# One core, attention at two scales and two feed-forward layers: v's tiles loaded per quarter of the partitions, block tails kept in SBUF, two weight tiles queued early, some decode and split work moved off VectorE

## The chip, the core and the metric

The kernel runs on one core of a Trainium2 chip. The metric is the device time of one execution in microseconds (us); of several executions the median is given. About 0.2% is what a measurement of this kernel can tell from no change.

## What is computed

The inputs q, k and v have 4 batches, 8 heads, 576 positions and 64 values a head. The attention is the sum of two: one over positions that are means of four neighbours (144 of them, full softmax, its output repeated four times), and one over a band of the seven nearest positions. Its output, 2304 tokens of 512 values, goes through two gated feed-forward layers.

```python
q_d, k_d, v_d = (t.reshape(B, H, S // 4, 4, D).mean(axis=3) for t in (q, k, v))
out_up = np.repeat(sm_attn(q_d, k_d, v_d), 4, axis=2)
mask = np.abs(pos[:, None] - pos[None, :]) < 4
out_local = softmax(where(mask, scale * q @ k.T, -1e9)) @ v
x = (out_up + out_local) as (B * S, H * D)
x = (sigmoid(x @ w_gate) * (x @ w_val)) @ w_out          # 512 -> 1536 -> 512
h = x @ w_in; x = (h * sigmoid(1.702 * h)) @ w_out2      # 512 -> 2048 -> 512
```

The weights arrive as 64-bit numbers (float64 bits) and are decoded on the chip.

## The kernel before, in words

**Units of work.** The tokens are cut into five blocks: block 0 to 3 are the first 512 tokens of each batch, block E gathers the last 64 tokens of each batch (its *tail*), 256 in all. The attention is cut into 16 *jobs*, one per batch and pair of heads (hp 0 to 3); jobs 0 to 3 make the input of block 0, jobs 4 to 7 that of block 1, and so on. A `Values` object holds v for two jobs (half of a batch's columns).

**A job** (`Job`). It loads qt and kt (288 KB each). `pools` makes the means of four on GpSimd (L462, L464) and of v on VectorE (L431, L433, from vg). `scores` multiplies in bands (TensorE L494), adds the mask (VectorE L501 into sc), takes the maximum, the exponential (ScalarE L512), normalizes and transposes (L521 into tt). `down` does the coarse attention (L534, L541, L549, L563), `down_t` transposes it (L578, L583 into pdt). `values` multiplies by v (L606 with vt, L614 with vd) and `combine` adds both parts into xf (L633), splits xf into a rounded high part xhi (ScalarE L638) and a rest xlo (VectorE L640), and, for the second half of the columns, writes the tail of 64 columns from xf to the DRAM buffer x1d.

**v's tiles** (`Values.load`). vt holds v in overlapping windows: 24 tiles of 32 rows, four of them on the four quarters of the partitions (32 partitions each) and six (g) behind each other. Before, one transfer brings one g for all quarters: eight transfers a half, of 96 to 128 partitions, and two small ones of 27.

**A feed-forward block** (`visit`). For each f (12 in layer 1, 16 in layer 2) `hidden` and `result` multiply: a group is three matmuls (L713, L714, L715: high by high, low by high, high by low), four groups for each of three weight tiles, 144 groups a block in layer 1. For block 0 each of the 36 weight tiles is loaded (512 KB), decoded (`bits`: scale, shift, or; `signed`: sign, into w32) and split into whi (ScalarE L677) and wlo (L679, VectorE for block 0, L679 on VectorE or GpSimd later). Blocks 1 to 3 use the decoded tiles again. Layer 2's tiles are decoded during block 3 and block E.

**What sets the order.** Every instruction is entered into a plan with its engine, an assumed duration, a due time and what it reads and writes. `Plan.order` then sets each engine's order by a simulation with these numbers; the engines run that order as it stands, each waiting at its own head. All loads and stores go through SP's queue in that order; a transfer waits for the one eight places before it. TensorE's gaps that the plan foresees are filled with matmuls on zeros (L885, `warm`).

Of the kernel before, what the change touches and what calls it, by code (L numbers as in the profile page):

```python
# [10 lines left out]
F32 = mybir.dt.float32  # L11
# [5 lines left out]
ALU = mybir.AluOpType  # L17
# [200 lines left out]
def tile_multiscale_attention_gated_ffn(  # L218
# [69 lines left out]
    ring("th", 2, [P, T])  # L288
    ring("ev", 2, [P, 512])
    ring("st", 2, [P, 512])  # L290
    ring("xf", 2, [P, HALF])


    wslots = ring("w", 3 * NF1, [P, 512], I32, wpool)
    aslots = []
    for nm, n, shape in (("qt", 2, [P, S + 12]), ("kt", 2, [P, KPAD + S + 5]), ("vt", 2, [P, NG, VC]),
                         ("sc", 2, [P, 2, NG, NU]), ("pt", 2, [P, 2, NG, 32]), ("tt", 2, [P, 2, NG, 32]),
                         ("vg", 1, [GH, 2, 4, VC]), ("half", 1, [P, G, 2]),
                         ("qd", 2, [P, G]), ("kd", 2, [P, G]), ("vd", 2, [GH, 2, VC]),
                         ("nm", 2, [P, 2, NG]), ("sm", 2, [P, 2, NG]), ("pd", 2, [GH, 2, 2, G]),  # L300
                         ("nmd", 2, [GH, 4]), ("smd", 2, [GH, 4]), ("pdt", 2, [GH, 2, 2, G]), ("up", 2, [P, G])):
# [19 lines left out]
        return [Buf(Slot(dram.tile([P, NK, T], F32, name=f"{name}_{j}", tag=f"{name}_{j}")))  # L321
                for j in range(len(blocks))]

    x1d, x2d = (dram_blocks(n) for n in ("x1d", "x2d"))


    warm = sb.tile([P, P], BF16, name="warm", tag="warm")
# [72 lines left out]
    class Values:  # L400
# [6 lines left out]
        def load(self):  # L407
            b, c = self.b, slice(self.c0, self.c0 + VC)
            self.vg, self.vt, self.vd = buf("vg"), buf("vt"), buf("vd")

            hp = self.job.hp
            d, after = (self.job.t0 - 3000.0, self.job.t0 - 12000.0) if b else (4500.0 * hp, 4500.0 * hp)
            for kh in range(2):
                dma(self.vg.t[:, kh], v[b, kh * 4 * GH:(kh + 1) * 4 * GH, c].rearrange("(g r) d -> g r d", r=4),
                    GH * 4 * VC * 4, [], [(self.vg, kh)], d, after)
            d, after = (self.job.due(0.2), self.job.t0 - 9000.0) if b else (4500.0 * hp + 3000.0, 6000.0 * hp)
            for g in range(NG):
                i0, i1 = g == 0, 4 - (g == NG - 1)
# [17 lines left out]
    class Job:  # L436
# [189 lines left out]

        def combine(self, a, z, s, xf, first, xh, xl):
            b, hp, up = self.b, self.hp, self.up
            m = z - a
            hi = min(z, T)  # L630
            at = self.due(0.9 if first else 1.0)
            part = (hp, first)
            op("dve", dve_ns(m), lambda: nc.vector.tensor_tensor(  # L633
                out=xf.t[:, :m].rearrange("p (g r) -> p g r", r=4),
                in0=s.t[:, :m].rearrange("p (g r) -> p g r", r=4),
                in1=up.t[:, a // 4:z // 4, None].to_broadcast([P, m // 4, 4]), op=ALU.add),
               [s, up], [xf], at)
            op("act", act_ns(hi - a), lambda: nc.scalar.copy(xh.t[:, hp, a:hi], xf.t[:, :hi - a]),  # L638
               [xf], [(xh, part)], at)
# [169 lines left out]

    def load_x(layer, j, t):  # L810
        n = width(j)
        src = (x1d if layer == 1 else x2d)[j]
        new_x((layer, j))
        direct.discard((layer, j))
        hi, lo = xs[layer, j]
        for k in range(NK):
            st = buf("st")
            reads = [(src, k)]
            if layer == 1:
                reads = [(src, (k, y)) for y in (range(B) if j == E else (True, False))]  # L820
            dma(st.t[:, :n], src.t[:, k, :n], P * 4 * n, reads, [st], t - 8000.0 + 500 * k)
            op("act", act_ns(n), lambda k=k, st=st: nc.scalar.copy(hi.t[:, k, :n], st.t[:, :n]),
               [st], [(hi, k)], t - 3000.0 + 500 * k)
            op("pool", pool_ns(n), lambda k=k, st=st: nc.gpsimd.tensor_sub(
                lo.t[:, k, :n], st.t[:, :n], hi.t[:, k, :n].bitcast(F32)),
               [st, (hi, k)], [(lo, k)], t - 3000.0 + 500 * k)
# [98 lines left out]
```

## Time and profile before

| | |
|---|---|
| median of 3 runs | 1001.41 us (1000.36 to 1001.48) |
| the profiled execution | 1000.16 us |
| its span, first to last instruction | 998.1 us |
| mean granted TensorE clock | 0.983 |
| TensorE busy | 961.1 us (96%) |
| VectorE busy | 526.0 us (53%) |
| ScalarE busy | 414.1 us (41%) |
| GpSimd busy | 219.1 us (22%) |

Busy times of TensorE count a matmul to its modelled end, and so hide short waits. Times inside the profile are counted from the start of the span.

### The profile page before, as it was taken

The numbers are of one execution on the slowest core, as the hardware profiler recorded it, in microseconds if no ns is written. First come the engines' busy times: TensorE is split into PE (matmuls) and PEld (weight loads), VectorE is DVE, ScalarE is ACT, GpSimd is POOL, SyncE is SP. The second block draws the span as 40 slices with busy tenths as digits, with TensorE's granted clock in tenths as the row PEclk, the third lists the DMA queues.
The fourth block names the chain that finished last, engine by engine and source line by source line (L and its number), as shares of the span: only waits on it lengthen the run. The fifth ranks groups of instructions, "written<-read, shape, count | busy, mean of one in ns | idle before, by whom it ended". The sixth has DMA issues, their size and how long they took to land.

```text
span 998.1 us, 18490 instructions
## 1 busy us (share of the span) xinstructions
PE 961.1 (96%) x7611; PEld 782.6 (78%) x7611; DVE 526.0 (53%) x932; ACT 414.1 (41%) x886; POOL 219.1 (22%) x212
## 2 busy tenths in 40 slices
PE   5799999899999999999999989999999999999997
PEld 5677677778778777888889967788888888888896
DVE  4899899554344544578655689523222222322232
ACT  2546565444444444555546555323223212322222
POOL 4111201333233332255435442102002000100000
PEclk8899999799999999999999999999999999999999
DMA  6656656130112110153105145002001000100010
GB/s 178 185 186 190 195 167 172 40 101 27 51 57 69 57 32 8 66 163 103 43 1 169 44 127 177 14 1 85 1 1 50 25 1 1 53 1 1 3 40 21
DMA packets 36931, 72.40 MB, mean 73 GB/s; under 512 B 5440, under 2 KB 17648, under 8 KB 36848
## 3 DMA queue, kind: packets, MB, share of 16 engines
q1 hardware_dynamic: 36848, 71.23, 22.9%
q8 instruction: 59, 0.97, 0.4%
q14 instruction: 24, 0.20, 0.1%
HBM read 61.26 MB, written 9.96 MB: 71 GB/s over the span
## 4 chain that ended last, share of the span: by engine, by line
PE 78%; DVE 13%; DMA 5%; issue 2%; ACT 1%; SPq 0%; DVEq 0%; ACTq 0%
PE ph L713 15%; PE ph L714 14%; PE ph L715 14%; PE acc L713 10%; PE acc L714 10%; PE acc L715 10%; DMA w<-w 3%; DVE we L666 3%; PE pa L606 2%; DVE we L671 2%; DVE w L671 1%; DVE we L664 1%; DVE wlo L679 1%; PE pa L494 1%; DMA x1d<-xf 1%
## 5 line engine op out<-in xcount | busy, mean ns | idle before, releaser
L749 DVE SCALAR_TENSOR_TENSOR th<-th,ph 128x512 f32<-128x512 f32 (+1 forms) x140 | 88.5, 632 | 282.2 <-ACT th L744 205.8
L744 ACT ACTIVATE th<-ph 128x512 f32<-128x512 f32 (+1 forms) x140 | 77.5, 554 | 259.7 <-PE ph L715 259.5
L713 PE MATMUL ph<-xhi,whi 128*128 128x512 f32 (+1 forms) x480 | 183.0, 381 | 0.4 <-ACT th L744 0.4
L714 PE MATMUL ph<-xhi,wlo 128*128 128x512 f32 (+1 forms) x480 | 178.9, 373 | 2.0 <-DVE wlo L679 2.0
L715 PE MATMUL ph<-xlo,whi 128*128 128x512 f32 (+1 forms) x480 | 177.9, 371 | 0.0
L679 POOL TENSOR_TENSOR wlo<-w,whi 128x512 fp32r<-128x512 f32 x90 | 121.1, 1345 | 239.2 <-ACT whi L677 234.7
L677 ACT CAST whi<-w 128x512 fp32r<-128x512 f32 x180 | 110.8, 617 | 106.9 <-PE acc L715 41.3
L713 PE MATMUL ph<-xhi,w 128*128 128x512 f32 (+1 forms) x320 | 120.0, 375 | 1.1 <-DVE th L749 0.9
L753 DVE TENSOR_TENSOR glo<-th,ghi 128x512 fp32r<-128x512 f32 (+1 forms) x140 | 95.6, 683 | 48.1 <-ACT ghi L752 47.6
L715 PE MATMUL ph<-xlo,w 128*128 128x512 f32 (+1 forms) x320 | 119.2, 372 | 0.0
L714 PE MATMUL ph<-xhi,w 128*128 128x512 f32 (+1 forms) x320 | 119.1, 372 | 0.0
L714 PE MATMUL acc<-w,glo 128*128 128x512 f32 x288 | 114.2, 397 | 2.5 <-DVE glo L753 2.5
L713 PE MATMUL acc<-w,ghi 128*128 128x512 f32 x288 | 113.9, 396 | 1.5 <-ACT ghi L752 1.5
L715 PE MATMUL acc<-w,ghi 128*128 128x512 f32 x288 | 114.0, 396 | 0.0
L752 ACT CAST ghi<-th 128x512 fp32r<-128x512 f32 (+1 forms) x140 | 80.8, 577 | 65.7 <-DVE th L749 63.1
L713 PEld LDWEIGHTS ph<-xhi,whi 128*128 128x128 f32 x480 | 91.1, 190 | 19.0 <-issue 3.9
L714 PEld LDWEIGHTS ph<-xhi,wlo 128*128 128x128 f32 x480 | 91.3, 190 | 17.7 <-DVE wlo L679 4.3
L715 PEld LDWEIGHTS ph<-xlo,whi 128*128 128x128 f32 x480 | 91.2, 190 | 15.5
L713 PE MATMUL acc<-ghi,whi 128*128 128x512 f32 (+1 forms) x240 | 91.0, 379 | 1.0 <-DVE ev L789 0.6
L714 PE MATMUL acc<-ghi,wlo 128*128 128x512 f32 (+1 forms) x240 | 89.2, 371 | 1.5 <-DVE wlo L679 1.5
L715 PE MATMUL acc<-glo,whi 128*128 128x512 f32 (+1 forms) x240 | 88.5, 369 | 0.5 <-DVE glo L753 0.5
L679 DVE TENSOR_TENSOR wlo<-w,whi 128x512 fp32r<-128x512 f32 x90 | 69.4, 772 | 19.2 <-ACT whi L677 19.1
(99 smaller groups left out, 1264.2 us busy)
## 6 DMA issues: line engine op xcount, KB each, us to landing
w<-w SPq DMA_DIRECT2D x68, 512.0 KB
qt<-qT SPq DMA_DIRECT2D x16, 288.0 KB
kt<-kT SPq DMA_DIRECT2D x16, 288.0 KB
vg<-v SPq DMA_DIRECT2D x16, 288.0 KB
vt<-v SPq DMA_DIRECT2D x32, 128.0 KB
x2d<-ev SPq DMA_DIRECT2D x16, 256.0 KB
st<-x2d SPq DMA_DIRECT2D x16, 256.0 KB
out<-ev SPq DMA_DIRECT2D x16, 256.0 KB
```

The costliest lines, as they stand in the source:

```text
L606: nc.tensor.matmul(s.t[h * D:(h + 1) * D, q:q + NQ], vt.t[ks, g, v0 + h * D:v0 + (h + 1) * D], tt.t[ks, h, g, :NQ], start=True, stop=True, ...
L666: op("dve", 602.0, lambda: nc.vector.scalar_tensor_tensor(e.t, wv[:, :, 0], 29, e.t, op0=ALU.logical_shift_right, op1=ALU.bitwise_or), [w] ...
L671: op("dve", 602.0, lambda: nc.vector.scalar_tensor_tensor(m.t, top, -2 ** 31, e.t, op0=ALU.bitwise_and, op1=ALU.bitwise_or), [w] if m is e ...
L677: op("act", 520.0, lambda: nc.scalar.copy(hi.t, m.t.bitcast(F32)), [m], [hi], due)
L679: op(eng, ns, lambda: on.tensor_sub(lo.t, m.t.bitcast(F32), hi.t.bitcast(F32)), [m, hi], [lo], due)
L713: nc.tensor.matmul(o, lhi, rhi, start=first, stop=False)
L714: nc.tensor.matmul(o, llo, rhi, start=False, stop=False)
L715: nc.tensor.matmul(o, lhi, rlo, start=False, stop=last)
L744: op("act", act_ns(n, True), lambda h=h: nc.scalar.activation(th.t[:, :n], h.t[:, :n], AF.Tanh, scale=0.5 if layer == 1 else 1.702 / 4.0), ...
L749: op("dve", dve_ns(n), lambda: nc.vector.scalar_tensor_tensor(th.t[:, :n], th.t[:, :n], 1.0, hb[-1].t[:, :n], op0=ALU.add, op1=ALU.mult), ...
L752: op("act", act_ns(n), lambda: nc.scalar.copy(gh.t[:, :n], th.t[:, :n]), [th], [gh], t)
L753: op("dve", dve_ns(n), lambda: nc.vector.tensor_sub(gl.t[:, :n], th.t[:, :n], gh.t[:, :n].bitcast(F32)), [th, gh], [gl], t)
```

## The change

1. vt is loaded by quarter of the partitions: four transfers of 32 partitions with five or six windows each, and two small ones of 28 and 27 partitions.
2. xf goes into the pool of the attention's buffers and no longer holds the tail; the tail's 64 columns are added by an instruction of their own into an SBUF buffer `tails` for all four batches. x1d is gone: block E's input is split straight from `tails`, without loads. sc has one buffer instead of two, which makes the room.
3. The first f's three weight tiles get due times of their own (`FIRST`), and the plan puts them among the first jobs' loads.
4. The first decode step (the scaling by 2 ** -112) is always on ScalarE; before, six tiles had it on VectorE (L660). For batch 0 the subtraction that makes xlo is on GpSimd.
5. The plan assumes 617 ns instead of 520 for ScalarE's operations of 512 columns.

```diff
-    ring("xf", 2, [P, HALF])
-                         ("sc", 2, [P, 2, NG, NU]), ("pt", 2, [P, 2, NG, 32]), ("tt", 2, [P, 2, NG, 32]),
+                         ("sc", 1, [P, 2, NG, NU]), ("pt", 2, [P, 2, NG, 32]), ("tt", 2, [P, 2, NG, 32]),
...
+                         ("xf", 2, [P, HALF])):
-    x1d, x2d = (dram_blocks(n) for n in ("x1d", "x2d"))
+    x2d = dram_blocks("x2d")
+    tails = Buf(Slot(sb.tile([P, NK, B * TAIL], F32, name="tails", tag="tails")))
...
-    E_DVE = 8.0e3
+    FIRST = ((-15.0e3, 0.0), (3.5e3, 0.0), (10.0e3, 8.0e3))
...
-            for g in range(NG):
-                i0, i1 = g == 0, 4 - (g == NG - 1)
-                src = v[b, NQ * (NG * i0 + g) - 3:NQ * (NG * i0 + g) + 29, c]
+            for i in (0, 2, 1, 3):
+                g0, g1 = i == 0, NG - (i == 3)
+                row = NQ * (NG * i + g0) - 3
+                src = v[b, row:row + 32, c]
                 src = bass.AP(tensor=src.tensor, offset=src.offset,
-                              ap=[[NG * NQ * DM, i1 - i0], [DM, 32], [1, VC]])
-                dma(self.vt.t[32 * i0:32 * i1, g], src, 32 * (i1 - i0) * VC * 4, [], [(self.vt, g)], d, after)
-            dma(self.vt.t[3:NU, 0], v[b, :NU - 3, c], (NU - 3) * VC * 4, [], [(self.vt, NG)], d, after)
+                              ap=[[DM, 32], [NQ * DM, g1 - g0], [1, VC]])
+                dma(self.vt.t[32 * i:32 * i + 32, g0:g1], src, 32 * (g1 - g0) * VC * 4, [], [(self.vt, i)],
+                    d, after)
+            dma(self.vt.t[3:NU + 1, 0], v[b, :NU - 2, c], (NU - 2) * VC * 4, [], [(self.vt, 4)], d, after)
...
-            op("dve", dve_ns(hi - a), lambda: nc.vector.tensor_sub(
-                xl.t[:, hp, a:hi], xf.t[:, :hi - a], xh.t[:, hp, a:hi].bitcast(F32)),
+            eng, ns, on = ("pool", pool_ns(m), nc.gpsimd) if b == 0 else ("dve", dve_ns(m), nc.vector)
+            op(eng, ns, lambda: on.tensor_sub(
+                xl.t[:, hp, a:hi], xf.t[:, :m], xh.t[:, hp, a:hi].bitcast(F32)),
                [xf, (xh, part)], [(xl, part)], at)
             if z > T:
-                dma(x1d[E].t[:, hp, b * TAIL:(b + 1) * TAIL], xf.t[:, T - a:m], P * 4 * (z - T),
-                    [xf], [(x1d[E], (hp, b))], at)
+                op("dve", dve_ns(z - T), lambda: add(tails.t[:, hp, b * TAIL:(b + 1) * TAIL], T, z),
+                   [s, up], [(tails, (hp, b))], at)
...
-        dma(w.t, (w1 if layer == 1 else w2)[f, part], P * 4096, [], [w], due - 5000.0, due - AHEAD)
+        at, after = due - 5000.0, due - AHEAD
+        if (layer, f) == (1, 0):
+            at, after = FIRST[part]
+        dma(w.t, (w1 if layer == 1 else w2)[f, part], P * 4096, [], [w], at, after)
...
-        if due < T0 + E_DVE:
-            op("dve", 335.0, lambda: nc.vector.tensor_scalar_mul(ef, wf[:, :, 1], 2.0 ** -112), [w], [e], due)
-        else:
-            op("act", 520.0, lambda: nc.scalar.activation(ef, wf[:, :, 1], AF.Copy, scale=2.0 ** -112),
-               [w], [e], due)
+        op("act", 617.0, lambda: nc.scalar.activation(ef, wf[:, :, 1], AF.Copy, scale=2.0 ** -112),
+           [w], [e], due)
```

The order of the instructions moves on every engine. Three places matter here.

SP's queue at the start of the kernel; qt and kt are a job's q and k, vg and vt are v, w a weight tile. Before:

```order
L367 DMA qt_137<-qT 128x576
L367 DMA kt_139<-kT 128x576
L367 DMA qt_138<-qT 128x576
L367 DMA kt_140<-kT 128x576
L367 DMA vg_149<-v 72x4x256 x2
L367 DMA vt_141<-v 96x1x256
L367 DMA vt_141<-v 128x1x256 x4
L367 DMA vt_141<-v 96x1x256
L367 DMA vt_141<-v 27x256 x2
L367 DMA qt_137<-qT 128x576
L367 DMA kt_139<-kT 128x576
```

and with the change:

```order
L368 DMA qt_135<-qT 128x576
L368 DMA kt_137<-kT 128x576
L368 DMA w_79<-w 128x512
L368 DMA qt_136<-qT 128x576
L368 DMA kt_138<-kT 128x576
L368 DMA vg_146<-v 72x4x256 x2
L368 DMA vt_139<-v 32x5x256
L368 DMA vt_139<-v 32x6x256 x2
L368 DMA vt_139<-v 32x5x256
L368 DMA vt_139<-v 28x256
L368 DMA vt_139<-v 27x256
L368 DMA w_80<-w 128x512
```

The first weight tile is now the third transfer and the second one stands ahead of the second pair's qt and kt, which follow it; v's half takes six transfers instead of eight.

VectorE after the scores of the first two jobs (sc scores, sm and pt softmax, we and w the decoding of weights). Before:

```order
L510 TENSOR_TENSOR sc_144<-sc_144,nm_158 128x360
L541 TENSOR_REDUCE nmd_164<-pa_177 72x2
L541 TENSOR_REDUCE nmd_164<-pa_178 72x2
L501 TENSOR_TENSOR sc_143<-acc_171,mask 128x180
L544 TENSOR_SCALAR nmd_164<-nmd_164 72x4
L501 TENSOR_TENSOR sc_143<-acc_173,mask 128x180
L513 TENSOR_REDUCE sm_160<-pt_146 128x12
```

and with the change:

```order
L513 TENSOR_TENSOR sc_141<-sc_141,nm_155 128x360
L547 TENSOR_SCALAR nmd_161<-nmd_161 72x4
L673 SCALAR_TENSOR_TENSOR we_83<-w_79,we_83 128x512
L671 TENSOR_SCALAR we_84<-we_84 128x512
L516 TENSOR_REDUCE sm_157<-pt_143 128x12
L519 TENSOR_SCALAR sm_157<-sm_157 128x12
L520 RECIPROCAL sm_157<-sm_157 128x12
```

Where VectorE had to wait for the scores of the third job (acc_171) before it could go on with job 1's softmax, steps of the first two tiles' decoding stand now, and that softmax comes ahead of the third job's scores.

VectorE at the end of job 1's values (xf the sum, xlo its rest). Before:

```order
L633 TENSOR_TENSOR xf_99<-pa_178,up_170 128x288
L633 TENSOR_TENSOR xf_100<-acc_172,up_170 128x288
L520 TENSOR_TENSOR pt_146<-pt_146,sm_160 128x12x30
L640 TENSOR_TENSOR xlo_87<-xf_99,xhi_85 128x288
L640 TENSOR_TENSOR xlo_87<-xf_100,xhi_85 128x224
L521 STREAM_TRANSPOSE tt_148<-pt_146 128x384
```

and with the change:

```order
L638 TENSOR_TENSOR xf_168<-acc_172,up_167 128x288
L638 TENSOR_TENSOR xf_169<-acc_173,up_167 128x224
L638 TENSOR_TENSOR tails<-acc_173,up_167 128x64
L544 TENSOR_REDUCE nmd_161<-acc_170 72x2
L544 TENSOR_REDUCE nmd_161<-acc_171 72x2
L547 TENSOR_SCALAR nmd_161<-nmd_161 72x4
```

The second addition stops at column 224 and the tail has its own; the two subtractions are no longer in VectorE's list.

## Rows read from the trace of the kernel before

**Rows 1.** The page's 40 slices of the span: granted TensorE clock in tenths.

```profile
PEclk8899999799999999999999999999999999999999
```

**Rows 2.** Stretches, only the matmuls of L713: us, PE busy (count), PEld busy (count), clock, DMA share, GB/s.

```profile
48.90:191.70 142.80, 60.69 (x144) 27.98 (x145) 0.95 0.53 163
191.70:309.90 118.20, 58.13 (x144) 26.98 (x144) 1.00 0.18 55
...
429.30:526.20 96.90, 55.71 (x144) 26.96 (x145) 1.00 0.23 77
```

**Rows 3.** Stretches: us; PE, PEld, DVE, ACT, POOL busy (count); clock, DMA share, GB/s.

```profile
0.00:10.00 10.00, 6.78 (x222) 6.29 (x223) 3.77 (x18) 1.28 (x1) 7.47 (x26) 1.00 0.65 191
...
0.00:60.00 60.00, 43.76 (x1149) 37.39 (x1151) 40.91 (x113) 23.49 (x77) 14.66 (x38) 0.83 0.63 192
60.00:175.00 115.00, 108.24 (x1141) 82.97 (x1137) 109.14 (x218) 65.17 (x149) 16.83 (x17) 1.00 0.57 176
176.00:186.00 10.00, 8.51 (x75) 6.23 (x76) 7.03 (x13) 4.41 (x10) 1.46 (x1) 0.52 0.01 2
191.70:310.00 118.30, 118.30 (x1202) 94.49 (x1201) 54.03 (x105) 55.25 (x133) 42.74 (x43) 1.00 0.18 55
...
30.00:33.50 3.50, 3.33 (x51) 2.83 (x49) 3.28 (x11) 1.98 (x7) 0.00 (x0) 1.00 0.96 296
45.50:48.50 3.00, 0.96 (x36) 0.96 (x40) 2.96 (x8) 1.82 (x6) 0.27 (x1) 0.53 0.26 84
```

**Rows 4.** The chain of work that ended last: start us, us, what.

```profile
3.68 6.01 DMA vg<-v
...
14.59 6.92 DMA kt<-kT
...
33.90 7.87 DMA x1d<-xf
...
59.40 0.67 DVE xlo L640 x2
...
166.53 9.52 DMA w<-w
```

**Rows 5.** Waits of VectorE, 0 to 60 us (three rows) and 60 to 192 us: total, times, longest.

```profile
DVE sc L501 <- PE acc L494: 6.5, 1, 6.5
DVE sc L501 <- PE pa L494: 3.4, 1, 3.4
DVE xf L633 <- DMA x1d<-xf: 2.3, 1, 2.3
...
DVE we L664 <- ACT we L662: 6.8, 3, 3.9
```

**Rows 6.** SP in order of time, 159 to 168 us: start us, us, issue.

```profile
159.52 6.91 SPq L367 DMA_DIRECT2D vt<-v  x5
166.53 1.30 SPq L367 DMA_DIRECT2D w<-w  x1
```

**Rows 7.** VectorE and GpSimd in order of time, 169.5 to 180 us.

```profile
170.36 1.35 POOL L679 TENSOR_TENSOR wlo<-w,whi 128x512 fp32r<-128x512 f32 x1 [7.63 <-ACT whi L677]
170.48 1.78 DVE L679 TENSOR_TENSOR wlo<-w,whi 128x512 fp32r<-128x512 f32 x1
...
177.96 0.69 DVE L679 TENSOR_TENSOR wlo<-w,whi 128x512 fp32r<-128x512 f32 x1
```

**Rows 8.** VectorE's groups by shape, 0 to 192 us: busy us, mean ns | idle before.

```profile
L501 DVE TENSOR_TENSOR sc<-pa,mask 128x180 f32<-128x180 f32 x13 | 4.1, 336 | 3.7 <-PE pa L494 3.4 <-ACT whi L677 0.4
L640 DVE TENSOR_TENSOR xlo<-xf,xhi 128x288 fp32r<-128x288 f32 x8 | 3.6, 450 | 0.0
...
L660 DVE TENSOR_SCALAR we<-w 128x512 f32<-128x512 f32 x6 | 3.2, 538 | 1.4 <-DMA w<-w 1.3
```

**Rows 9.** GpSimd in order of time, 22 to 25 us.

```profile
22.89 0.66 POOL L462 TENSOR_TENSOR half<-qt 128x288 f32<-128x288 f32 x1
```

**Rows 10.** TensorE in order of time, 165 to 195 us; in brackets its idle time before.

```profile
177.50 0.69 PE L578 MATMUL pa<-ident,pd 72*72 72x72 f32 x4 [4.19 <-DVE sc L501]
```

More of the change, by code (lines that the diff above doesn't have):

```diff
@@ L300, in tile_multiscale_attention_gated_ffn @@
                          ("nm", 2, [P, 2, NG]), ("sm", 2, [P, 2, NG]), ("pd", 2, [GH, 2, 2, G]),
-                         ("nmd", 2, [GH, 4]), ("smd", 2, [GH, 4]), ("pdt", 2, [GH, 2, 2, G]), ("up", 2, [P, G])):
+                         ("nmd", 2, [GH, 4]), ("smd", 2, [GH, 4]), ("pdt", 2, [GH, 2, 2, G]), ("up", 2, [P, G]),
+                         ("xf", 2, [P, HALF])):
         aslots += ring(nm, n, shape, F32, apool)
@@ L416, in load @@
             d, after = (self.job.due(0.2), self.job.t0 - 9000.0) if b else (4500.0 * hp + 3000.0, 6000.0 * hp)
-            for g in range(NG):
-                i0, i1 = g == 0, 4 - (g == NG - 1)
-                src = v[b, NQ * (NG * i0 + g) - 3:NQ * (NG * i0 + g) + 29, c]
+            for i in (0, 2, 1, 3):
+                g0, g1 = i == 0, NG - (i == 3)
+                row = NQ * (NG * i + g0) - 3
+                src = v[b, row:row + 32, c]
                 src = bass.AP(tensor=src.tensor, offset=src.offset,
-                              ap=[[NG * NQ * DM, i1 - i0], [DM, 32], [1, VC]])
-                dma(self.vt.t[32 * i0:32 * i1, g], src, 32 * (i1 - i0) * VC * 4, [], [(self.vt, g)], d, after)
-            dma(self.vt.t[3:NU, 0], v[b, :NU - 3, c], (NU - 3) * VC * 4, [], [(self.vt, NG)], d, after)
+                              ap=[[DM, 32], [NQ * DM, g1 - g0], [1, VC]])
+                dma(self.vt.t[32 * i:32 * i + 32, g0:g1], src, 32 * (g1 - g0) * VC * 4, [], [(self.vt, i)],
+                    d, after)
+            dma(self.vt.t[3:NU + 1, 0], v[b, :NU - 2, c], (NU - 2) * VC * 4, [], [(self.vt, 4)], d, after)
             row = NQ * (NT - 1) - 3
-            dma(self.vt.t[96:96 + S - row, NG - 1], v[b, row:S, c], (S - row) * VC * 4, [], [(self.vt, NG + 1)],
+            dma(self.vt.t[96:96 + S - row, NG - 1], v[b, row:S, c], (S - row) * VC * 4, [], [(self.vt, 5)],
                 d, after)
@@ L628, in combine, with add @@
             b, hp, up = self.b, self.hp, self.up
-            m = z - a
             hi = min(z, T)
+            m = hi - a
             at = self.due(0.9 if first else 1.0)
             part = (hp, first)
[L633 to L638, printed above, removed]
+            def add(out, o0, o1):
+                nc.vector.tensor_tensor(
+                    out=out.rearrange("p (g r) -> p g r", r=4),
+                    in0=s.t[:, o0 - a:o1 - a].rearrange("p (g r) -> p g r", r=4),
+                    in1=up.t[:, o0 // 4:o1 // 4, None].to_broadcast([P, (o1 - o0) // 4, 4]), op=ALU.add)
+            op("dve", dve_ns(m), lambda: add(xf.t[:, :m], a, hi), [s, up], [xf], at)
+            op("act", act_ns(m), lambda: nc.scalar.copy(xh.t[:, hp, a:hi], xf.t[:, :m]),
                [xf], [(xh, part)], at)
-            op("dve", dve_ns(hi - a), lambda: nc.vector.tensor_sub(
-                xl.t[:, hp, a:hi], xf.t[:, :hi - a], xh.t[:, hp, a:hi].bitcast(F32)),
+            eng, ns, on = ("pool", pool_ns(m), nc.gpsimd) if b == 0 else ("dve", dve_ns(m), nc.vector)
+            op(eng, ns, lambda: on.tensor_sub(
+                xl.t[:, hp, a:hi], xf.t[:, :m], xh.t[:, hp, a:hi].bitcast(F32)),
                [xf, (xh, part)], [(xl, part)], at)
             if z > T:
-                dma(x1d[E].t[:, hp, b * TAIL:(b + 1) * TAIL], xf.t[:, T - a:m], P * 4 * (z - T),
-                    [xf], [(x1d[E], (hp, b))], at)
+                op("dve", dve_ns(z - T), lambda: add(tails.t[:, hp, b * TAIL:(b + 1) * TAIL], T, z),
+                   [s, up], [(tails, (hp, b))], at)
     wt = {}
@@ L675, in parts_of @@
     def parts_of(m, hi, lo, due, eng):
-        op("act", 520.0, lambda: nc.scalar.copy(hi.t, m.t.bitcast(F32)), [m], [hi], due)
+        op("act", 617.0, lambda: nc.scalar.copy(hi.t, m.t.bitcast(F32)), [m], [hi], due)
         ns, on = (602.0, nc.vector) if eng == "dve" else (1230.0, nc.gpsimd)
@@ L811, in load_x @@
         n = width(j)
-        src = (x1d if layer == 1 else x2d)[j]
         new_x((layer, j))
@@ L816, in load_x @@
         for k in range(NK):
-            st = buf("st")
-            reads = [(src, k)]
             if layer == 1:
[L820 to L826, printed above, removed]
+                st, x, reads = tails, tails.t[:, k], [(tails, (k, b)) for b in range(B)]
+            else:
+                st, reads = buf("st"), None
+                x = st.t[:, :n]
+                dma(x, x2d[j].t[:, k, :n], P * 4 * n, [(x2d[j], k)], [st], t - 8000.0 + 500 * k)
+                reads = [st]
+            op("act", act_ns(n), lambda k=k, x=x: nc.scalar.copy(hi.t[:, k, :n], x),
+               reads, [(hi, k)], t - 3000.0 + 500 * k)
+            op("pool", pool_ns(n), lambda k=k, x=x: nc.gpsimd.tensor_sub(
+                lo.t[:, k, :n], x, hi.t[:, k, :n].bitcast(F32)),
+               [*reads, (hi, k)], [(lo, k)], t - 3000.0 + 500 * k)
     def visit(v_):
```

## The prediction

> **What bounds the kernel now.** Start with the granted clock in the 40-slice view [rows 1]. It reads 8 in the first two slices (0 to 50 us), 7 in the eighth (175 to 200 us) and 9, which stands for full, everywhere else. The clock falls where TensorE stands still, so these are the places to look at.
>
> Next, how long each block of 512 tokens takes in the first layer [rows 2]. Every block is the same 144 groups of three matmuls. Block 3 has no attention beside it and takes 96.9 us, 0.67 us a group. Block 1 shares TensorE with the attention of block 2 and takes 118.2 us. Block 0 shares it with the attention of block 1, the same work, and takes 142.8 us, and it only begins at 48.9 us. So what can be saved lies before 191.7 us: 24.6 us inside block 0, and part of the 48.9 us ahead of it.
>
> Third, the engines in stretches [rows 3]. From 60 to 175 us VectorE is busy 109.14 of 115 us: it decodes the 36 weight tiles of layer 1 there, and it sets the pace. From 0 to 60 us it works only 40.91 us, so 19.1 us are idle. In block 1 TensorE is busy 118.30 of 118.30 us: from there on a microsecond won earlier is kept, and one spent on another engine costs nothing.
>
> Fourth, what VectorE waited for [rows 5] and the chain of work that ended last [rows 4]. Before 60 us: 6.5 and 3.4 us for score matmuls, 2.3 us for the write of a block tail, 1.3 us for the first weights [rows 8]. On the chain stand three transfers: kt issued at 14.59 us takes 6.92 us, the tail's write of 32 KB takes 7.87 us, a weight tile of 512 KB issued at 166.53 us takes 9.52 us.
>
> Fifth, why transfers are slow. While weights are loaded the DMA engines are 0.96 busy at 296 GB/s; while SP issues v's tiles (45.5 to 48.5 us) the DMA engines are 0.26 busy at 84 GB/s [rows 3]. A quarter of the engines carries v's tiles, and what is queued on that quarter behind them waits. The last weight tile of block 0 is issued right behind five v tiles whose issue alone took 6.91 us [rows 6].
>
> **The change, part by part.**
>
> v's tiles. Per half of v 759 KB (0.78 MB) move, 9.3 us at 84 GB/s. The new shape is in no row; its bounds are 84 and 296 GB/s, 9.3 and 2.6 us. I take the 191 GB/s of the first 10 us, in which all kinds of loads are mixed [rows 3]: 4.1 us. Ahead of kt of the second pair of jobs stand then 3.41 MB of q, k, v's groups and two weight tiles (11.5 us at 296 GB/s) and 4.1 us of v; six loads before the first v tiles (1.77 MB, 6.0 us) landed at 9.7 us (3.68 + 6.01) [rows 4], so I count from 3.7 us: 19.3 us, against 21.5 (14.59 + 6.92). VectorE's 6.5 us wait [rows 5] shrinks to some 3, since weight decode now stands in it: **-3.5 us**.
> A rule speaks against this part. The Trainium skill, page "SBUF — State Buffer", section "Door 1: The DMA port swizzle", says that a transfer to 32 partitions reaches 8 of 16 ports and measures 189 GB/s where 128 partitions measure 328. No row here shows such a transfer of v. Scaled to this case's 296 GB/s it would be 171 GB/s and 4.6 us a half, and the sum would be 0.5 us smaller.
>
> Tails on the chip. 16 writes of 32 KB and 4 loads leave SP, whose own time nothing waits for: 0. The wait of 2.3 us [rows 5] goes, because the buffer xf is no longer held by a DMA: **-2.3 us**. 16 additions of 64 columns come to VectorE, each between 0 and the 0.336 us of a 180-column addition [rows 8]; I take 0.2. Four fall into the front and four into the decode stage: +0.8 us each. The other eight lie beside TensorE-bound blocks, where VectorE works 54 of 118 us [rows 3]: nothing. If that cover went they would cost 1.6 us.
>
> First weights between the jobs. Two tiles are queued among the first q, k and v, two more before the third pair. The 1.3 us wait goes: **-1.3 us**. Their 1.05 MB cost 3.5 us of transfer, which is already in the 19.3 us above. The waits that this adds: ScalarE's second operation now waits for the first tile, and VectorE's first decode step, ahead of its first scores, waits for ScalarE. The tile is third in the queue; with it 1.11 MB have come at 3.7 + 3.8 = 7.5 us, so that job 0's softmax begins up to 1.5 us later. Its result is used only behind kt of the third job, at 19.3 us: 0, and without that slack +1.5 us. The second tile's step stands ahead of job 1's softmax; it lands before kt, for which TensorE waits anyway: 0.
>
> Work off VectorE. Six scalings move to ScalarE at 0.538 us each [rows 8], five of them before 60 us: **-2.7 us**; ScalarE works 23.49 of 60 us there [rows 3] and has room. Eight subtractions move to GpSimd at 0.45 us each [rows 8]: -3.6 us. What comes back: beside a GpSimd operation of 1.35 us a VectorE subtraction took 1.78 us instead of 0.69 [rows 7], so 1.1 us was lost. A GpSimd pass over 288 columns takes 0.66 us [rows 9]; eight can cost VectorE from 0 to 5.3 us. I take +2 us, since the decode operations that would be hit are few in that stretch.
> The Trainium skill, on the same page, section "Who interferes with whom", has this as a lock: a VectorE instruction with two SBUF inputs and a GpSimd instruction that reads SBUF exclude each other. Rows 7 agree (1.78 is 0.69 + 1.09); by the lock alone the move would give 3.6 and take up to 5.3 back, and the sum would be 3.3 us smaller.
>
> Front, to the end of job 3's values (59.40 + 0.67 = 60.07 us, [rows 4]): -3.5 - 2.3 - 1.3 - 2.7 - 3.6 + 0.8 + 2 = **-10.6 us**.
>
> Decode stage. VectorE's 6.8 us waits for ScalarE [rows 5] are waits for weights behind v's tiles (three times, the longest 3.9). A tile of 512 KB needs 1.8 us at 296 GB/s; I keep 1.8 us of the 6.8: -5; one scaling -0.5; tails +0.8: **-4.7 us**.
>
> The clock. At 177.50 us TensorE had waited 4.19 us [rows 10], which follows from that late weight; then the granted clock is 0.52 for 10 us (176 to 186 us) [rows 3], which is nearly all of it at the 1.2 GHz level, and 4.8 us of work are lost. If TensorE does not stop, the clock does not fall: **-4.8 us**.
>
> The score buffer sc goes from two to one: a job's scores then wait until the exponential of the job before has read them; in the new order another job's values stand between, so 0, at most 2 us. Loads of x2d are now issued between its writes: SP can stand some us there, behind it the next q and k, used a job later: 0, covered by 118.30 of 118.30 us.
>
> Sum: -10.6 - 4.7 - 4.8 = -20.1 us. The profiled execution took 1000.16 us (span 998.1), so 980.1; the median of the runs, 1001.41, is 1.25 above it: **981 us**. Test of it: block 1 would begin at 171.6 us. TensorE alone needs the 118.2 us of block 1 from job 3's values on (60.07 - 10.6 = 49.5), so it could begin at 167.7: VectorE still sets the pace, barely.
>
> **Rivals.**
> TensorE becomes the bound. For it: in 60 to 175 us it works 108.24 of 115 us already [rows 3]. If transfers come at 296 GB/s and the front shrinks by 15 us, block 1 starts at 45 + 118 = 163 us, 28 us earlier: 973 us.
> v's tiles land no faster, because smaller pieces of the partitions keep to few DMA engines as the old ones do. Nothing in the trace excludes it; against it, a tile of 128 partitions need not be slow (0.96 for weights), so the cause lies in the old tiles' shape. The 3.5 us of two early weights are then added to kt's 21.5 us, and the decode and clock terms stay away: -2.3 - 1.3 - 6.3 + 2.8 + 3.5 = -3.6, 998 us. (The Trainium skill, page "DMA: Bandwidth & Descriptors", section "Rules for kernel authors", says that splitting a transfer by partitions brings nothing, since the pieces serialize.)
> Slower: the early weights push q and k back. The place is SP's queue, where two tiles stand ahead of the second pair's kt and ScalarE and VectorE wait for them in order. The price is one us per us that kt lands after 21.5 us. The other terms of the front (7.1 us) are used up when kt lands at 28.6 us, two more make it slower by over 0.2%; v's tiles at 84 GB/s and the weights at the same rate (12.5 us) would do it: kt at 34.0 us, 12.5 - 7.1 = 5.4 us more, 1007 us. Against it: weights move at 296 GB/s.
> The move to GpSimd gives nothing (lock): 984 us, inside the range.
>
> **How the numbers follow.** My sum 0.61; the lock 0.08; TensorE bound 0.13; v no faster 0.13; slower 0.05. The range is 969 (the TensorE case with 4 us of extra front) to 993 (of the sum only the front, with 2 us of it missing); the v case and the slower case, 0.18, fall out. About 0.2% is what a measurement of this kernel can tell. Faster 0.92 (all but slower and a little of the v case), same 0.03, slower 0.05.
>
> **What would show it.** Right: no wait for x1d, a DMA share well above 0.26 while v's tiles move, kt of the second pair landing before 20 us, job 3's values done near 49 us, weight tiles landing in under 5 us, no half clock after the first 50 us, block 1 starting near 171 us, and blocks 1 to 3 and layer 2 as long as now. Wrong: v's tiles at 84 GB/s; or VectorE idle for ScalarE in the decode stage; or block 1 later than 180 us; or the gain given back after 191 us.

## The result, and the profile after

The changed kernel takes 984.84 us (median of 4 runs, 984.09 to 988.31), the kernel before beside it 1000.88 us: a ratio of 0.9849 (95% interval 0.9822 to 0.9876), 16.0 us less. That is 3.8 us above the forecast of 981.0 and inside its range. The sum behind it held in two of its three stages and failed in the third: the decode stage and the clock gave what they should, the front gave nothing in the profile.

The profiled execution took 988.31 us, 3.5 us above the median of its four runs, so the traces below explain 11.6 us (span 998.1 to 986.5) of the 16.

The page's 40 slices after the change, granted TensorE clock and busy share of the DMA engines in tenths ([rows 1] before):

```profile
PEclk8579999999999999999999999999999999999999
DMA  9736757332104300042104154002002000100010
```

The digit 7 of the eighth slice is gone; the second and third slices are lower than before. On record TensorE is at the low level (0.5) for 41.0 us before block 1, before it was 30.7: the low clock left the decode stage and grew in the front.

Stretches with only the matmuls of the same line (now L720): block 0, block 1, block 3 ([rows 2] before; us, PE and PEld busy and count, clock, DMA share, GB/s):

```profile
56.06:181.25 125.19, 59.47 (x144) 27.70 (x145) 0.97 0.60 173
181.25:300.76 119.51, 58.30 (x145) 27.02 (x144) 1.00 0.22 57
420.26:516.90 96.64, 55.59 (x145) 26.98 (x144) 1.00 0.22 71
```

Block 0 takes 125.2 instead of 142.8 us, but begins at 56.1 instead of 48.9. Blocks 1 and 3 are as long as before. Block 1 begins at 181.25 instead of 191.7 us, 10.5 us earlier; the forecast said 171.6. From there to the end it is 805.3 us, before 806.4.

The engines by stretch ([rows 3] before; us, then PE, PEld, DVE, ACT, POOL busy and count, clock, DMA share, GB/s):

```profile
10.00:20.00 10.00, 5.73 (x134) 4.89 (x135) 5.62 (x16) 2.82 (x12) 1.70 (x4) 0.66 1.04 214
20.00:30.00 10.00, 5.83 (x177) 4.87 (x177) 6.09 (x17) 5.17 (x19) 4.68 (x8) 0.59 1.01 206
0.00:60.00 60.00, 47.27 (x1137) 40.10 (x1138) 37.26 (x101) 24.22 (x79) 21.49 (x44) 0.68 0.73 181
60.00:175.00 115.00, 113.67 (x1126) 89.31 (x1125) 113.02 (x227) 70.57 (x161) 20.31 (x20) 0.99 0.64 184
176.00:186.00 10.00, 10.00 (x164) 8.21 (x158) 5.43 (x13) 4.79 (x9) 4.78 (x5) 1.00 0.01 2
...
38.60:43.20 4.60, 4.60 (x104) 3.77 (x105) 1.16 (x4) 2.39 (x11) 0.39 (x2) 0.50 0.83 195
```

From 60 to 175 us VectorE is busy 113.02 of 115 us (109.14 before) and TensorE 113.67: there is little left to wait for. From 176 to 186 us TensorE is at full clock (0.52 before). But from 0 to 60 us VectorE works 3.7 us less than before (37.26 against 40.91) in the same 60 us: it is idle 22.7 us instead of 19.1. The work that was taken from it brought no time there: by 60 us it had even done less of the decoding (7.9 us of it, before 10.1, the scalings left out). From 10 to 30 us the DMA engines are full, and move only 206 to 214 GB/s. The last row is a stretch in which SP issues five of v's tiles: 195 GB/s at 0.83, where the old tiles had 84 GB/s at 0.26.

What VectorE waited for, 0 to 60 us (three rows) and 60 to 182 us (total, times, longest; [rows 5] before):

```profile
DVE xf L638 <- PE acc L609: 10.5, 3, 5.1
DVE we L671 <- ACT we L669: 5.2, 1, 5.2
DVE vg L434 <- DMA vg<-v: 4.3, 1, 4.3
...
DVE we L671 <- ACT we L669: 0.5, 2, 0.3
```

The old waits for scores (9.9 us) and for the tail's write (2.3) are gone but for 0.6. Three others stand in their place: for the first weight tile, which is now decoded ahead of the first scores (5.2), for v's groups (4.3), and for the first jobs' values (10.5). The chain of work that ended last (start us, us, what; [rows 4] before) and VectorE in order of time show why:

```profile
3.09 10.47 DMA vg<-v
...
13.57 7.26 DMA w<-w
...
26.29 4.56 issue
...
101.45 3.61 DMA w<-w
```

```profile
15.50 1.22 DVE L434 TENSOR_TENSOR vg<-vg 72x1024 f32<-72x1024 f32 x1 [4.31 <-DMA vg<-v]
```

The first of v's two groups takes 10.47 us; the second, issued at 4.15 us, is there at 15.4. The 6.01 us of [rows 4] are those of the second. So VectorE begins with both at 15.50 us, before at 9.78. The softmax of the first jobs stands behind it on VectorE, ScalarE waits for that, and TensorE's values for ScalarE. The third row of the chain is a stop of TensorE in the middle of one job's values, with no wait for data (more on it at the end). The last is the one weight tile on the chain from 60 us to block 1: 3.61 us, where the chain of before has 9.52 at the end of the stage.

### The profile page after: what moved, and what is told of

Same layout as the page of the kernel before. It is cut to its first block, busy times and chain, and to the rows that moved or that the text cites. A ratio compares the mean times of both kernels' runs of the same rounds, so it can differ in the third digit from the quotient of the medians.

```text
span 986.5 us, 18428 instructions
## 1 busy us (share of the span) xinstructions
PE 963.1 (98%) x7612; PEld 786.5 (80%) x7612; DVE 521.6 (53%) x934; ACT 416.1 (42%) x892; POOL 228.6 (23%) x220
## 4 chain that ended last, share of the span: by engine, by line
PE 84%; DVE 9%; DMA 2%; issue 2%; ACT 1%; SPq 0%; DVEq 0%; ACTq 0%
PE ph L720 16%; PE ph L721 15%; PE ph L722 15%; PE acc L720 11%; PE acc L721 10%; PE acc L722 10%; DVE we L673 2%; PE pa L609 2%; DVE we L678 1%; DMA w<-w 1%; DMA vg<-v 1%; PE pa L497 1%; PE acc L609 1%; DVE we L671 1%; PE pa L537 1%
## 5 line engine op out<-in xcount | busy, mean ns | idle before, releaser
L720 PE MATMUL ph<-xhi,whi 128*128 128x512 f32 (+1 forms) x480 | 182.4, 380 | 0.2 <-DVE th L756 0.2
L720 PE MATMUL ph<-xhi,w 128*128 128x512 f32 (+1 forms) x320 | 119.7, 374 | 0.6 <-DVE th L756 0.2
L760 DVE TENSOR_TENSOR glo<-th,ghi 128x512 fp32r<-128x512 f32 (+1 forms) x140 | 94.0, 672 | 48.6 <-ACT ghi L759 48.3
L720 PE MATMUL acc<-w,ghi 128*128 128x512 f32 x288 | 114.3, 397 | 2.9 <-ACT ghi L759 1.5
L720 PEld LDWEIGHTS ph<-xhi,whi 128*128 128x128 f32 x480 | 90.9, 189 | 19.5 <-issue 4.3
L720 PE MATMUL acc<-ghi,whi 128*128 128x512 f32 (+1 forms) x240 | 90.6, 378 | 0.2 <-DVE ev L796 0.2
L832 POOL TENSOR_TENSOR xlo<-st,xhi 128x512 fp32r<-128x512 f32 (+1 forms) x20 | 26.0, 1315 | 219.0 <-ACT xhi L830 218.8
```

The lines of the kernel that those rows point to most:

```text
L720: nc.tensor.matmul(o, lhi, rhi, start=first, stop=False)
L760: op("dve", dve_ns(n), lambda: nc.vector.tensor_sub(gl.t[:, :n], th.t[:, :n], gh.t[:, :n].bitcast(F32)), [th, gh], [gl], t)
L832: op("pool", pool_ns(n), lambda k=k, x=x: nc.gpsimd.tensor_sub(lo.t[:, k, :n], x, hi.t[:, k, :n].bitcast(F32)), [*reads, (hi, k)], [(lo, k ...
```

## The experiments

Each kernel was timed against the kernel before on the same chip; "block 1" is the start of its first group in that kernel's profile. The plan orders everything anew for each edit, so a microsecond of difference can be its doing. The last column is the time of the profiled execution: it lies up to 4.7 us from the median, and "block 1" belongs to it.

| kernel | median us | ratio (95% interval) | block 1 | profiled us |
|---|---|---|---|---|
| the change | 984.84 | 0.9849 (0.9822 to 0.9876) | 181.2 | 988.3 |
| 1 v as before | 992.29 | 0.9909 (0.9894 to 0.9923) | 184.7 | 991.6 |
| 2 no early weights | 986.59 | 0.9856 (0.9838 to 0.9874) | 178.5 | 985.5 |
| 3 only v's tiles | 988.54 | 0.9866 (0.9848 to 0.9884) | 177.7 | 985.9 |
| 4 work back on VectorE | 984.51 | 0.9828 (0.9812 to 0.9843) | 178.0 | 984.6 |
| 5 v in one transfer | 983.04 | 0.9819 (0.9801 to 0.9838) | 175.3 | 982.2 |
| 6 the same in quarters | 986.20 | 0.9847 (0.9828 to 0.9865) | 179.2 | 986.0 |
| 7 plan at 200 GB/s | 983.53 | 0.9821 (0.9806 to 0.9835) | 176.8 | 983.4 |
| 8 twice the fillers | 991.97 | 0.9896 (0.9880 to 0.9913) | 187.0 | 993.8 |
| 9 = 5, plan at 230 GB/s | 981.67 | 0.9801 (0.9777 to 0.9825) | 170.2 | 977.4 |
| 10 fewer fillers | 987.63 | 0.9858 (0.9835 to 0.9881) | 182.3 | 989.1 |
| 11 first tile behind v's groups | 983.52 | 0.9826 (0.9799 to 0.9853) | 181.2 | 988.2 |
| 12 = 9 and 11 | 980.09 | 0.9787 (0.9767 to 0.9808) | 176.4 | 983.9 |

In every profile 804.7 to 806.4 us lie between the start of block 1 and the end of the span. Nearly all differences are made before it.

**1 and 3: v's tiles undone, and v's tiles alone.** In 1 the loop over `g` of before stands again (six transfers of 96 to 128 partitions a half, with the two small ones eight); 3 is the kernel before with the loop over `i`.

```diff
-            for i in (0, 2, 1, 3):
-                g0, g1 = i == 0, NG - (i == 3)
+            for g in range(NG):
+                i0, i1 = g == 0, 4 - (g == NG - 1)
```

> The changed kernel with v's tiles loaded as before (eight transfers of 96 to 128 partitions a half). Theory V (the gain of about 16 us is the decode stage's, and comes from v's new tiles, since weight tiles no longer queue behind them): block 0 goes back from 125 us to 138 us or more, weight tiles with over 5 us of landing return, 996 to 1004 us. Rival W (the gain comes from the work taken off VectorE): 985 to 990 us, block 0 stays near 125 us.

> The kernel before with v's tiles by quarters of the partitions, and nothing else changed. Theory V: block 0 near 128 us instead of 142.8, the clock drop at 176 us gone, 985 to 991 us. Rival W: 996 to 1001 us.

v's tiles alone give 13.1 us, the rest of the change alone 9.4, both together 16.0. Neither theory held for run 1: 992.3 lies between the two. For run 3 theory V held (988.5; block 0 takes 131.1 us, near its 128). On top of v's tiles the rest is worth 2.9 us by the medians, 1.7 by the ratios, and the intervals overlap: v's tiles are nearly the whole of the gain. The parts overlap by 6.5 us, and two stretches bear on it: without v's tiles (first and second row), and with them alone (third and fourth), 60 to 175 and 176 to 186 us.

```profile
60.00:175.00 115.00, 110.97 (x1060) 86.61 (x1060) 108.86 (x219) 67.97 (x156) 17.86 (x19) 0.98 0.56 176
176.00:186.00 10.00, 10.00 (x137) 8.16 (x138) 7.48 (x13) 4.25 (x9) 3.12 (x2) 1.00 0.17 50
```

```profile
60.00:175.00 115.00, 111.74 (x1249) 87.03 (x1248) 113.71 (x229) 69.15 (x159) 20.52 (x18) 1.00 0.60 172
176.00:186.00 10.00, 10.00 (x46) 8.29 (x45) 5.07 (x7) 4.05 (x7) 6.38 (x7) 1.00 0.26 85
```

The low clock behind 176 us, 4.8 us of work, is gone in both, so either part alone removes it, as far as one trace of each can show. VectorE's pace in the decode stage is v's doing alone: 113.71 of 115 us with the new tiles, 108.86 (as in [rows 3]) without. Its wait for weights behind 60 us is 0.2 us in run 3 and 4.4 us in run 1 (6.8 in [rows 5]).

**2 and 11: the early weights.** In 2 the first f's tiles have the due times of all others again; in 11 the first tile is queued behind v's groups.

```diff
-        if (layer, f) == (1, 0):
-            at, after = FIRST[part]
```

```diff
-    FIRST = ((-15.0e3, 0.0), (3.5e3, 0.0), (10.0e3, 8.0e3))
+    FIRST = ((1.0e3, 0.0), (10.0e3, 8.0e3), (10.0e3, 8.0e3))
```

> The changed kernel without the due times of its own for the first three weight tiles. Theory F (the early weights push q, k and v's groups back, the rival of the prediction): the first group of block 0 comes 5 to 8 us earlier (48 to 51 us instead of 56), 977 to 980 us. Rival R (the front is bound by the rate at which all its bytes come, 181 to 214 GB/s, whatever the order): first group within 3 us of 56, 983 to 988 us.

> The changed kernel with the first weight tile queued behind v's groups instead of third, the second and third still early. Theory F2 (the tile third in the queue costs VectorE 5.2 us of waiting for it and 4.3 us more for v's groups): v's groups land before 11.5 us, the two waits together fall from 9.5 to below 4 us, block 1 begins 3 to 6 us earlier, 979 to 982 us. Rival (what is saved there is waited for later, as the time of block 1 is set by all the bytes and by TensorE): waits move, 983 to 987 us.

Without early weights block 0's first group comes at 49.3 us, as theory F said, yet the time, 986.6, is that of rival R. In its profile VectorE works 40.97 of the first 60 us and block 1 begins 2.7 us earlier; but the profiled executions, 985.5 us and 988.3 in the change, differ by as much, and not the way the medians do. Why the earlier block 0 brings nothing by the medians is not shown. With the tile behind v's groups VectorE begins with these at 12.11 us, 3.4 us earlier (not before 11.5, as theory F2 had it), and its wait for the tile is gone, but others take its place: VectorE, 0 to 60 us, of 11.

```profile
DVE xf L638 <- PE acc L609: 6.2, 2, 3.5
DVE vg L434 <- DMA vg<-v: 5.1, 2, 3.6
DVE sc L504 <- PE pa L497: 3.3, 1, 3.3
```

The two waits fell from 9.5 to 5.1 us, not below 4, and block 1 begins no earlier in its profile (of 988.2 us, 4.7 above the median). 983.5 us lies in the rival's range; its interval reaches into both. In this front early weights are worth nothing measurable, for or against.

**4: the scalings of the first tiles and batch 0's subtractions back on VectorE.**

```diff
-            eng, ns, on = ("pool", pool_ns(m), nc.gpsimd) if b == 0 else ("dve", dve_ns(m), nc.vector)
+            eng, ns, on = "dve", dve_ns(m), nc.vector
...
+        if due < T0 + E_DVE:
+            op("dve", 335.0, lambda: nc.vector.tensor_scalar_mul(ef, wf[:, :, 1], 2.0 ** -112), [w], [e], due)
```

> The changed kernel with the early scalings and batch 0's subtractions back on VectorE. Theory V: VectorE has idle time in the front (37.3 of 60 us busy), so only what falls behind 56 us counts: 984 to 988 us. Rival W: the 6.3 us of the two moves and more come back, 991 us or above. Prediction's lock term: taking the subtractions off GpSimd gives up to 2 us back.

984.5 us, in the range of theory V: the part of the change that takes work off VectorE is worth nothing measurable. VectorE is busy 40.95 of the first 60 us here and 37.26 in the change: what it does not do in the front it only waits longer for. The run undoes both moves at once, so it does not tell the idle time from what GpSimd's subtractions take from VectorE.

**5 and 6: how v's bytes come.** The host lays v out in the windows of vt, zeros at both ends (a copy of rows); 5 loads a half in one transfer to 128 partitions, 6 in four of 32, both with 6 KB a row. VectorE's four small zero fills of vt go in both.

```diff
+            dma(self.vt.t, vw[b, hp // 2], P * NG * VC * 4, [], [self.vt], d, after)
```

```diff
+            for i in (0, 2, 1, 3):
+                r = slice(32 * i, 32 * i + 32)
+                dma(self.vt.t[r], vw[b, hp // 2][r], 32 * NG * VC * 4, [], [(self.vt, i)], d, after)
```

> The changed kernel with v laid out on the host as vt wants it (windows, zeros at both ends), so that a half of v is one transfer to all 128 partitions, 6 KB from each row. Theory D (the front, 0 to 60 us, stayed as long as before because the quarter transfers keep the DMA engines full at only 206 to 214 GB/s): 10 to 30 us move at 260 GB/s or more, block 1 begins at 170 to 175 us instead of 181, 974 to 979 us. Rival C (the front is lost to TensorE's half clock, 41 us of it before block 1): more bandwidth alone leaves it, 982 to 986 us.

> As the run with v laid out on the host, but each half as four transfers of 32 partitions. Theory P (32 partitions at a time reach only some of the ports, which is what makes the packets slow): 10 to 30 us stay near 210 GB/s with the engines full, 983 to 987 us. Rival Q (pieces of 1 KB were slow, which are 6 KB here): as fast as the single transfer, within 2 us of it.

10 to 20 us, the single transfer and then the quarters:

```profile
10.00:20.00 10.00, 8.71 (x199) 7.41 (x201) 7.84 (x21) 5.73 (x22) 4.03 (x5) 0.66 0.99 324
```

```profile
10.00:20.00 10.00, 6.66 (x149) 5.70 (x149) 6.64 (x19) 3.98 (x15) 1.17 (x2) 0.81 1.06 228
```

The same rows of the same 6 KB: 324 GB/s in one piece, 228 in quarters, both with full engines. So theory P holds: it is the 32 partitions that make the packets slow (in the median a packet of 6 KB took 236 ns in 5, 420 ns in 6), not the size of the pieces. That several transfers follow each other does not slow them by itself: the weights move so at 296 GB/s [rows 3]. 6 is no faster than the change, 5 is 3.2 us faster than 6 by the medians (the intervals overlap). But the median of 5, 983.0, lies where rival C put it, 1.8 us below the change, although 324 GB/s move from 10 to 20 us: the rate alone was not what held it.

The Trainium skill, page "SBUF — State Buffer", section "Door 1: The DMA port swizzle", gives 189 GB/s for 32 partitions against 328 for 128; these two rows agree with it in direction: the ratio is 0.70 here and 0.58 there, with other loads mixed in here.

**7, 8, 10: order and fillers.** 7 gives the plan the rate that the trace shows; 8 and 10 change the assumed length of a filler (110 ns). The traces have 172 fillers in the change, 347 in 8 and 83 in 10; the 86 and 60 of the expectation for 10 are not in them.

```diff
-                dma = max(dma, t) + o.ns / self.DMA_RATE
+                dma = max(dma, t) + o.ns / (200.0 if t < 40.0e3 else self.DMA_RATE)
```

```diff
-    WARM_NS = 110.0
+    WARM_NS = 55.0      (8)      220.0      (10)
```

> The changed kernel with the plan reckoning 200 GB/s instead of 300 up to 40 us, which is what the trace shows there: the order and the fillers then fit the landings. Theory E (the second early weight tile, 7.3 us on its way, holds ScalarE for 5.9 us, and job 1's values and TensorE behind it): that wait goes, block 1 begins 3 to 8 us earlier, 977 to 982 us. If order does not matter: 983 to 987 us.

> The changed kernel with fillers counted at 55 ns instead of 110 ns, so that TensorE's foreseen gaps are filled with twice as many matmuls on zeros. Rival C: less than 25 us of half clock before block 1 instead of 41, 976 to 981 us. Theory D: the gaps are waits for transfers that the plan does not foresee, the half clock stays, 983 to 988 us.

> The changed kernel with fillers counted at 220 ns: 60 instead of 86 matmuls on zeros in the front, the order of all else unchanged. Theory I (TensorE runs ahead of the loading of its own instructions, and stands some 4.6 us in the front until 16 KB of them land; doubling the fillers gave three such gaps): no more than one such gap, 982 to 985 us, not slower than the changed kernel. Rival C (fillers keep the clock up): more than 41 us of half clock before block 1, 987 us or more.

In 7 VectorE's waits for the first tile and for v's groups (0.4 us left) and TensorE's long stop are gone, and VectorE works 45.03 of the first 60 us; block 1 begins 4.4 us earlier in the profile, as theory E had it, but the median, 983.5, is below the change by 1.3 us only, in the range of "order does not matter", and the intervals overlap. Theory E named the wrong tile: the 5.9 us are ScalarE's wait for the first tile, for the second it stands 0.4 us. That order matters is likely from the profile, its size is not shown.

8 is 7 us slower than the change, above both of its ranges, with less low clock before block 1 (23.9 us against 41.0, as rival C asked). TensorE's waits, 0 to 60 us:

```profile
PE acc L893 <- issue: 4.9, 2, 4.2
PE acc L609 <- issue: 4.2, 1, 4.2
PE acc L497 <- issue: 3.6, 1, 3.6
```

Three stops of about 4 us instead of one; the kernels with the old filler length have none to two. That more fillers (L893) make more stops is likely, not shown. 10 is the counter-test, and shows a trap. Its page has the clock at 9 from the first slice on and 1.00 from 0 to 60 us, but its timeline, TensorE around 63.6 us, has the three matmuls of a group start 0.43 us apart, and then 0.23:

```profile
62.46 0.63 PE L720 MATMUL ph<-xhi,whi 128*128 128x512 f32 x1
62.88 0.63 PE L721 MATMUL ph<-xhi,wlo 128*128 128x512 f32 x1
63.31 0.54 PE L722 MATMUL ph<-xlo,whi 128*128 128x512 f32 x1
63.69 0.40 PE L720 MATMUL ph<-xhi,whi 128*128 128x512 f32 x1
63.92 0.39 PE L721 MATMUL ph<-xhi,wlo 128*128 128x512 f32 x1
```

The trace's first record of the clock is at 63.6 us, and the page shows full clock where no record stands. Up to there TensorE ran at the lower of its two levels (1.2 and 2.4 GHz): the fillers of this front start 107 ns apart, as they do in the change where the record says low, against 56 ns where it says full. By its number, 987.6, the run lies where rival C put it and not where theory I did (982 to 985), though it has one long stop only (5.6 us). But with the clock low for the whole front, against 41.0 us on record in the change, the median is only 2.8 us more, and the intervals overlap: the low clock of the front costs little, if anything.

**9 and 12: the parts joined.** 9 joins 5 and 7 (at 230 GB/s), 12 adds the order of 11.

> v as one transfer a half and the plan reckoning 230 GB/s up to 40 us, together. If both remove front time of their own (transfers, and waits out of order), their gains add: block 1 begins near 172 us, 977 to 980 us. If they remove the same time, or TensorE's half clock is what is left: 981 to 984 us, as each alone.

> v as one transfer a half, the plan reckoning 230 GB/s up to 40 us, and the first weight tile queued behind v's groups. Theory F2: VectorE's first wait of 6.5 us for the tile (as it was with the first two alone) goes and little takes its place, so block 1 begins 2 to 5 us earlier than there (170.2 us in its profile, 981.7 us): 976 to 980 us. Rival (what is saved at the start is waited for later): 980 to 984 us.

12 takes 980.1 us, 2.1% less than the kernel before (ratio 0.9787, 0.9767 to 0.9808) and clearly less than the change; it lies at the border of its two ranges. 9, 981.7, lies in its second range, and its interval reaches into both; block 1 at 170.2, which fits the first, belongs to an execution of 977.4 us. VectorE's waits, 0 to 60 us, of 9 and then of 12:

```profile
DVE we L658 <- ACT we L656: 6.5, 1, 6.5
DVE sc L491 <- PE acc L484: 3.1, 1, 3.1
DVE xf L625 <- PE pa L596: 1.4, 1, 1.4
DVE vg L421 <- DMA vg<-v: 1.3, 1, 1.3
```

```profile
DVE sc L491 <- PE acc L484: 6.7, 3, 3.6
DVE sc L491 <- PE pa L484: 5.6, 1, 5.6
DVE xf L625 <- PE pa L596: 3.5, 2, 2.9
```

The wait of 6.5 us for the tile is gone in 12 and 9.2 us of waits for scores are new. The median is 1.6 us lower than in 9, with overlapping intervals. The profiles are of executions of 977.4 us (9) and 983.9 us (12), so that most of what is saved at the start is waited for later is likely, not shown.

## Why the prediction was right, and where its steps failed

By its own sum, in the profiled execution: front -10.6 forecast, 0 measured (VectorE is done with job 3's values at 60.2 us, before at 60.1; their subtraction, now on GpSimd, ends at 62.5); from there to block 1, -9.5 forecast (decode -4.7, clock -4.8), -10.5 measured (131.6 us to 121.1); behind block 1, 0 forecast, -1.2 measured. By the medians 4 to 5 us more were won than in this execution; which stage they belong to, the one trace does not show. Of its signs of being right, the wait for x1d is gone, v's tiles move at 0.83, the weight tile on the chain took 3.61 us, and the rest is as long as before; kt before 20 us, job 3's values near 49 us and no low clock behind 50 us (0.62 up to 60) did not come. One sign of being wrong came: block 1 later than 180 us (181.25, in an execution 3.5 us above the median).

- **Decode stage and clock: right together.** VectorE's wait for weights went from 6.8 to 0.5 us, the low clock behind 176 us is gone, and VectorE sets the pace from 60 us on, as the sum said. How the 10.5 us divide between the two terms is not shown. v's tiles alone were priced at 3.5 + 5.0 + 4.8 = 13.3 us; run 3 gave 13.1.
- **"Six scalings to ScalarE -2.7, eight subtractions to GpSimd -3.6, +2 back": wrong.** Measured: nothing beyond noise (run 4). The prediction knew that VectorE was idle 19.1 of the front's 60 us and still counted its work as path. This is the largest single step that failed, 4.3 us.
- **"Its step is used only behind kt, 0" (the first weight tile): wrong.** The tile stands third in the queue and its decoding ahead of the first scores on VectorE, which stood 5.2 us for it; v's groups came later and cost 4.3 more. The prediction looked only at who uses the result, not at what stands behind the waiting instruction.
- **"kt of the second pair lands at 19.3 us": wrong.** Its q was only there at 22.04 us, when GpSimd could begin (before at 20.29; the prediction's own test said kt before 20):

```profile
22.04 0.81 POOL L465 TENSOR_TENSOR half<-qt 128x288 f32<-128x288 f32 x1 [9.07 <-DMA qt<-qT]
```

  SP issued it at 15.48 us, when v's second group, eight places ahead, had landed. Without the early weights (run 2) it was there at 17.65. The sum took 296 GB/s for q, k and weights beside v's tiles, where the trace shows 206 to 214 for everything together. The prediction gave the slow transfers to 32 partitions 0.5 us, for v's own bytes; they slowed what was in flight with them too: with v over all partitions VectorE begins with v's groups at 12.71 us instead of 15.50. Run 5, with v over all partitions, began block 0 at 44.1 us instead of 56.1, though only part of that reached the end.
- **Tails: right in price, short in gain.** The additions take 0.21 us (estimate 0.2). The wait for x1d is gone, as is the 1.3 us for the first weights of before, but others took their place. Kernels with the tails on the chip need 1 us less behind block 1 (804.7 to 805.7 against 806.4 in the kernel before and in run 3); the forecast had nothing there. No run takes the tails, the single score buffer or the 617 ns back by themselves, so which of them that is, and what they are worth, is not shown.
- **GpSimd's subtraction** takes 1.02 us in the mean of 0.79 to 1.14 where 0.66 was read from a pass that adds, and VectorE's sum of v's groups, beside two of them, took 1.82 instead of 1.22 us. What VectorE lost beside all eight is some 2.9 us, an estimate from its operations there against the same ones elsewhere: near the +2 of the sum, far from 5.3.

```profile
L647 POOL TENSOR_TENSOR xlo<-xf,xhi 128x288 fp32r<-128x288 f32 x4 | 4.1, 1015 | 18.8 <-ACT xhi L644 18.8
...
L638 DVE TENSOR_TENSOR tails<-pa,up 128x64 f32<-128x64 f32 x5 | 1.1, 210 | 0.0
```

The rivals: TensorE did not become the bound alone (113.67 beside VectorE's 113.02 of 115 us); v's tiles do land faster; the early weights and v's tiles do push other loads back, as the slower rival said, but most on v's groups, and the other terms were larger. The lock's 984 us is the nearest number, but it loses 3.3 us of the front where all 10.6 were lost. That the forecast came out near is partly luck: the decode stage and the clock carried the gain, as forecast, but the front's 10.6 us, more than half of the forecast gain, did not come in the profile, and 1.2 us behind block 1 and the 4 to 5 us that the medians add, neither of them in the sum, stand in their place.

## What to carry to other kernels

Count work taken off an engine only in stretches where that engine is busy; where it waits, first name what it would wait for next. A transfer queued early can cost whoever is in flight with it, and an instruction that waits for it holds up all that stands behind it on its engine, however late its result is used. Check the rate that a planner assumes against the trace: with a rate near the real one, v over all partitions and the first weight tile behind v's groups (run 12, v laid out on the host), this kernel gained a further 4.8 us.

## What the runs showed of the hardware

**TensorE's stops end just after a packet of instructions lands.** The page's queue named instruction moves 60 packets, 0.98 MB, over the span: one of 16 KB per 254 of TensorE's 15224 matmuls and weight loads.

```profile
q8 instruction: 60, 0.98, 0.4%
```

The stop of 4.56 us from 26.29 to 30.85 us waits for no data. The DMA answers for 26.3 to 28.0 us hold no packet of that queue; those for 28.0 to 29.5 us hold one:

```profile
q1 hardware_dynamic: 267, 0.33, 98.1%
q8 instruction: 1, 0.02, 5.5%
```

It landed at 29.42 us and TensorE went on 1.43 us later. All sixteen stops of over 2 us that the traces of these fourteen kernels put down to nothing else before 60 us, 2.5 to 6.7 us long, end in this way, 1.3 to 1.65 us after such a packet landed; the other 103 of the 119 packets that landed in these stretches ended no such stop. Run 8, with more instructions in the front, had three. It is read from the packets' times; an experiment that changes only the instructions' loading was not made, nor is it shown that data ahead of a packet make it late.

**The old v tiles kept about four of the sixteen DMA engines at work.** From 46.0 to 48.3 us of the kernel before 3 to 6 packets were in flight at any time, 4 in 60% of it; 0.26 of 16 is 4.2. With the new tiles 0.83 of 16 is 13.

**Full engines are no full rate.** The DMA engines' share was 1.04 at 214 GB/s with v in quarters and 0.99 at 324 GB/s with v in one piece; a share near 1 says nothing of the rate.

**A clock of 1.00 can be the lack of a record.** In run 10 only the spacing of equal matmuls told the level, 0.43 and then 0.23 us for 512 columns.
